# Filter transform: two stacked products become one of 128 columns; the last chunk is scored by VectorE

## The chip, the cores and the metric

One core of a Trainium2 chip runs the whole program. The metric is the device time of one execution in microseconds; a kernel is judged by the median of several executions. TensorE multiplies matrices out of on-chip memory into its accumulators (PSUM, eight banks), VectorE (DVE), ScalarE (ACT) and GpSimd (POOL) do elementwise work, and SyncE (SP) issues most of the transfers to and from device memory. All data are float32.

## The reference

A long convolution with a gate, followed by a small mixture of experts. The filter is made from a table of positions by two small products, then windowed.

```python
h_filt = (np.maximum(pos_emb @ w1, 0.0) @ w2) * np.exp(-0.01 * pos)[:, None]
u = x * v
Hf = np.fft.rfft(h_filt, n=2 * S, axis=0)             # S = 12608, 128 channels
Uf = np.fft.rfft(u, n=2 * S, axis=1)                  # 4 batches
y = np.fft.irfft(Uf * Hf[None], n=2 * S, axis=1)[:, :S]
x = x * y
# per batch: the 128 rows with the highest scores go through one expert
scores = np.einsum('bsd,d->bs', x, w_gate)
top = np.argpartition(-scores[b], 128)[:128]
out[b, top] = x[b, top] + sigmoid(scores[b, top]) * (np.maximum(x[b, top] @ w1, 0) @ w2)
```

## The kernel before

The transforms are done as real (Hartley) transforms of length 101 x 250, written as matrix products. Channels go through in 32 groups of four (`NG`), and everything is placed by hand: buffers lie at fixed offsets of one large tile (`arena`, another is `big`), and each engine works its instructions off in the order in which the program issues them. There is no scheduler and no table that sets the order.

**The filter** comes first. `h_hid` makes it in `big` (`hb`: 101 rows, two versions e = 0 and 1, 128 channels, 126 columns). `h_spec` then transforms it, group by group, and writes the spectrum to device memory (`hd`, L409), from where the main loop reads it for each batch. A group passes through these steps:

- `fold` (L365): the 126 columns are folded about their middle, sum and difference of column j and column 125 - j, for both e and four channels: two operations of 504 elements a row. VectorE does the first four groups, GpSimd the rest, four groups ahead, in four buffers (`fbo`).
- `fwd`, the first stage (L380): for each e and channel two products of 101 rows, 63 columns of weights (the folded filter) and 101 moving columns (`c1_sb`), one for rows 0 to 62 of the output, the other for rows 64 to 126. Which of the two, sum or difference, stands above is exchanged between e = 0 and 1 (`w ^ e`), so that for the second stage all that goes to p is above and all that goes to q below. Then ScalarE copies the two outputs to `te` (L383).
- The second stage (L400): for two halves of the moving columns, e and w, a product of 63 rows, 64 columns of weights (`fo_sb`, a table of cosines and sines) and 202 moving columns: eight a group. Row half w goes to bank p or q, e to the column half.
- ScalarE copies q (L402), VectorE makes the spectrum in four operations of 404 (L405, L406, twice L408), and SP sends it off (L409). The buffer written by L408 is one of two, so that L408 waits for the transfer of two groups before.

On TensorE, `fwd` of group g + 1 stands ahead of the second stage of group g. PSUM is double-buffered for both stages: the first uses banks a0 and a1 for even groups and c1 for odd ones, the second c2 and c0.

**The main loop** (128 steps, four batches of 32 groups) does the same for the input: `f_s1` (L424) and `dft` (L266) on TensorE, the product with the spectrum on VectorE (L430 to L445), `f_sd` on GpSimd, the way back `f_i` (L261) on TensorE.

**At the end of a batch** `P1.run` finishes the convolution in 32 steps h over the rows of the output (`mm`: L541, L545), multiplies by x (`fin`: L556) and scores. For scoring a chunk of up to four positions is multiplied by the gate vector (`weigh`, L590, by VectorE or, where `far`, by GpSimd) and ScalarE sums each position (`sums`, L600). In the last batch only, the last step (h = 31, two positions) is scored in one operation a position by VectorE (L574), under `end`. In that batch PSUM banks rotate among three (`ring`), h = 30 in a0, h = 31 in a1; the first expert's products for three batches (`Experts.half`, through L257) go to a0 and then a1 right behind, then eight warming products (L794), four products of the second expert layer (L257), and then the first count of the search for the 128 highest scores, which goes on in 16 rounds between VectorE and TensorE. A product is two records, each with its weight load, in the trace.

Of the kernel before, what the change touches and what calls it, by code (L numbers as in the profile page):

```python
# [17 lines left out]
B, S, D, FO = 4, 12608, 128, 64  # L18
NQ = 64
# [20 lines left out]
JH = (N3 + 1) // 2  # L40
# [51 lines left out]
def _tables():  # L92
    kap = np.arange(N1) - N1 // 2
    idx = _grid()
    r1, r3 = idx[:, 0] % N1, idx[0] % N3
    rho, chi = (-1.0) ** np.arange(N1), (-1.0) ** (np.arange(N3) + r3)
    c1 = np.zeros((128, 1 + NB, N1))
    c1[:N1, 0] = _cas(r1[:, None] * kap[None, :], N1)
    alt = rho[:, None] * c1[:N1, 0]
    for k, (c, lo, hi) in enumerate(_steps()[1]):  # L100
        c1[:hi, 1 + k], c1[hi:N1, 1 + k] = alt[:hi], -alt[hi:]
        c1[N1:N1 + hi - lo, 1 + k] = -2 * alt[lo:hi]
    g = _cas(kap[:, None] * N2 * np.arange(GW)[None, :], N1)
    gx = _split(np.concatenate([g, -g], axis=1))
    r = np.arange(NK)
    cf = np.zeros((N3, 2, 2, NQ))
    for e in range(2):
        ang = 2.0 * np.pi * ((r3[:, None] * (2 * r + e)[None, :]) % N2) / N2
        cf[:, 0, e, :NK] = np.cos(ang)
        cf[:, 1, e, :NK] = np.sin(ang)  # L110
    j = np.arange(NJ)
    ci = np.zeros((128, 2, NJ))
    for e in range(2):
        k = 2 * r + e
        wk = np.where((k == 0) | (k == N3), 0.5, 1.0)[:, None] / (2 * N)
        ang = 2.0 * np.pi * ((k[:, None] * j[None, :]) % N2) / N2
        ci[e * NQ:e * NQ + NK, 0] = np.cos(ang) * wk
        ci[e * NQ:e * NQ + NK, 1] = np.sin(ang) * wk
    fold = np.zeros((128, 2, NQ))
    fold[:JH] = cf[:JH, 0]  # L120
    fold[NQ:NQ + JH] = cf[:JH, 1]
    cf[:, :, 1] *= chi[:, None, None]
    win = np.exp(np.float32(-0.01) * np.arange(N1 * N3, dtype=np.float32))
    sg = np.where(idx % N2 < N3, 1.0, -1.0).astype(np.float32)
    wm = np.zeros((PR, 3, N3), np.float32)
    wm[:N1, 0] = np.where(idx < S, win[idx], 0.0)
    wm[:N1, 1] = sg
    wm[:, 2] = wm[:, 0] * wm[:, 1]
    p = np.arange(128)
    tk = np.zeros((128, 2 * 128 + 2 + 36 + NJ + 40), np.float32)  # L130
    tk[:, :128] = p[:, None] < p[None, :]
    tk[:, 128:256] = p[None, :]
    tk[:, 256] = NJ * np.clip(p - P0, 0, PR - 1)
    tk[:, 257] = p + 1
    steps = np.array([[i << sh for i in range(4)] for sh in range(14, -1, -2)])
    steps = np.concatenate([steps, steps[:1] - 32768])
    tk[:, 258:294] = steps.reshape(1, -1)
    tk[:, 294 + NJ:] = np.concatenate([-steps[:8], 0.5 - steps[8:], 0.5 - steps[:1]]).reshape(1, -1)
    tk[:, 294:294 + NJ] = np.where(_valid(), -NEG, NEG)
    f = np.float32  # L140
    cf = np.concatenate([cf.reshape(N3, 4, NQ), np.zeros((128 - N3, 4, NQ))])
    return (fold.astype(f), c1.astype(f), gx.astype(f), cf.astype(f), ci.astype(f), wm, tk)
# [18 lines left out]
def hyena_moe(ctx, tc, xg, x2, pos, bw, ww, wg, mw1, mw2, fo, c1, gx, cf, ci, wm, tk, out):  # L161
# [61 lines left out]
    nc.vector.memset(onesb, 1.0)  # L223
    ay = view(big, 0, [128, NG, 2 * NJ, 4])
    hb = view(big, 0, [N1, 2, D, N3 + 1])
    fo_sb = view(arena, OFF["wx"][0] + 32 * JH, [128, 2, NQ])
    fbo = [OFF["wx"][0], OFF["wx"][0] + 16 * JH] + [OFF["xa"][0] + k * 8 * D for k in (2, 3)]
    hd = dp.tile([128, NG, 2 * HC], F32, name="hd")
    blk = [c for c, _, _ in _steps()[1]]

# [121 lines left out]
    def h_spec():  # L352
        te = {}

        def tps(g):
            if g % 2:
                t = ps2(1, [128, 2, 512], f"htp_{g}")
                return [t[:, e, :HC] for e in range(2)]
            return [ps1(e, [128, HC], f"htp_{g}_{e}") for e in range(2)]

        def pqs(g):
            t = ps2(0 if g % 2 else 2, [128, 2, 512], f"hpq_{g}")
            return [t[:, e, :HC] for e in range(2)]

        def fold(g, eng=nc.gpsimd):  # L365
            if g >= NG:
                return
            fb[g] = view(arena, fbo[g % 4], [N1, 2, 2, 4, JH])
            hg = hb[:, :, 4 * g:4 * g + 4]
            for k, op in enumerate((ALU.add, ALU.subtract)):  # L370
                eng.tensor_tensor(out=fb[g][:, k], in0=hg[:, :, :, :JH], in1=hg[:, :, :, N3:JH - 1:-1], op=op)

        def fwd(g):
            b = fb.pop(g)
            tp = tps(g)
            t = te[g] = buf("te", g, [128, 2, HC])
            for e in range(2):
                for s in range(4):
                    for w in range(2):
                        nc.tensor.matmul(tp[e][w * NQ:w * NQ + JH, s * N1:(s + 1) * N1], lhsT=b[:, w ^ e, e, s], rhs=c1_sb[:N1, 0],  # L380
                                         start=True, stop=True)
            for e in range(2):
                nc.scalar.copy(out=t[:, e], in_=tp[e])  # L383
            fold(g + 4)

        fb = {}
        for g in range(4):
            fold(g, nc.vector)
        fwd(0)
        for g in range(NG):  # L390
            if g + 1 < NG:
                fwd(g + 1)
            p, q = pqs(g)
            t = te.pop(g)
            for h in range(2):
                c = slice(h * 2 * N1, (h + 1) * 2 * N1)
                for e in range(2):
                    for w, o in enumerate((p, q)):
                        r = slice(w * NQ, w * NQ + JH)
                        nc.tensor.matmul(o[e * NQ:(e + 1) * NQ, c], lhsT=fo_sb[r, e], rhs=t[r, e, c], start=True, stop=True)  # L400
            qs = buf("qs", g, [128, HC])
            nc.scalar.copy(out=qs, in_=q)  # L402
            vs = buf("yz", g, [128, HC])
            ht = buf("sd", g, [128, 2, HC])
            nc.vector.tensor_tensor(out=nat(vs), in0=rev(p), in1=nat(qs), op=ALU.subtract)  # L405
            nc.vector.tensor_tensor(out=nat(p), in0=nat(p), in1=rev(qs), op=ALU.add)  # L406
            for e, op in enumerate((ALU.add, ALU.subtract)):
                nc.vector.tensor_tensor(out=ht[:, e], in0=p, in1=vs, op=op)  # L408
            nc.sync.dma_start(hd[:, g], ht.rearrange("p e c -> p (e c)"))  # L409
            if NG - 5 <= g < NG - 3:  # L410
                stage_u(g - NG + 5)
                load_u(g - NG + 7)
            if g == NG - 2:
                stage_u(2)
            if g >= NG - 3:
                load_h(g - NG + 3)
# [83 lines left out]
    class P1:  # L500
# [47 lines left out]
        def fin(self, h):  # L548
            ja, n = self.hbs[h]
            blk = ja // 8  # L550
            xa = self.xa[blk]
            js = slice(ja % 8, ja % 8 + n)
            end = self.last and n == 2
            if end:
                self.weigh()
            nc.vector.tensor_tensor(out=xa[:, js], in0=self.s4.pop(h)[:, :n], in1=xa[:, js], op=ALU.mult)  # L556
            if not end:
                self.weigh()
                far = ja >= JM and n == HB and h not in DW
                if h >= NL and not self.last:  # L560
                    o = OFF["cm"][0] + 2 * NC * D if h < 30 else OFF["wx"][0]
                    wx = view(arena, o + h % 2 * HB * D, [128, HB, D])
                elif far:
                    wx = view(arena, CE[self.pw % 2], [128, HB, D])
                    self.pw += 1
                else:
                    wx = view(arena, self.wx[self.nw % 4], [128, HB, D])
                    self.nw += 1
                self.mul = xa[:, js], wx[:, :n], ja, n, far, h
                if far:  # L570
                    self.weigh()
            else:
                for k in range(n):
                    nc.vector.scalar_tensor_tensor(out=junk, in0=xa[:, ja % 8 + k], scalar=1.0,  # L574
                                                   in1=self.wg, op0=ALU.mult, op1=ALU.mult,
                                                   accum_out=self.sc[:, ja + k:ja + k + 1])
            if ja + n == blocks[blk][1]:
                j0, j1 = blocks[blk]
                nc.sync.dma_start(out[self.b, :, j0:j1], xa[P0:P0 + PR, :j1 - j0])
                i = ORD.index(blk)  # L580
                if i:
                    self.load_a(i - 1 + NX + len(XE))
                if blk in CB:
                    self.comb()
# [573 lines left out]
```

## Time and profile before

| | |
|---|---|
| median of three executions | 905.29 us (904.11 to 909.53) |
| profiled execution | 909.53 us, span 907.8 us |
| busy of the span | TensorE 869.9 us (96%), VectorE 808.5 (89%), GpSimd 763.5 (84%), ScalarE 626.6 (69%) |
| filter made (`h_hid`) | up to about 34.7 us |
| filter transformed (`h_spec`) | 34.7 to about 120.5 us |
| main loop with the ends of the first three batches | to about 840 us |
| end of the fourth batch, search, experts | to 907.8 us |

The profiled execution is the longest of the three; the profile's times are of this one. In the lines of the profile, a line starts with the source line, the engine and the operation, then the tile written, an arrow and the tiles read, the shape (for a product: rows of weights x columns of weights, then rows and columns moving), and the number of instructions; behind a bar stand busy time in us, the mean of one in ns and the idle time just before with what ended it. Timeline lines start with start and length in us. `PEld` is TensorE's loading of weights, which can run beside its products; ends of products are modelled. "c", "a", "arena", "big" are the tiles of the program without their numbers.

### The profile page before, as it was taken

How to read it: one execution, taken by the hardware profiler on the slowest of the kernel's cores; microseconds unless marked ns; L12 is line 12 of the kernel's file. 1: busy time of each engine (PE TensorE's matmuls, PEld its weight loads, DVE VectorE, ACT ScalarE, POOL GpSimd, SP SyncE). 2: the span in 40 equal slices, each digit the busy share in tenths (PEclk: the TensorE clock that was granted, in tenths of full speed). 3: DMA queues.
4: the chain of work that ended last, by engine and by line, in shares of the span. 5: the costliest groups of instructions: out<-in, count | busy, mean ns of one | idle time of the engine just before them, and what ended most of it. 6: DMA issues, size and time to landing. Idle time of an engine off the chain costs nothing.

```text
span 907.8 us, 46386 instructions
## 1 busy us (share of the span) xinstructions
PE 869.9 (96%) x19606; PEld 760.9 (84%) x19606; DVE 808.5 (89%) x1543; ACT 626.6 (69%) x2238; POOL 763.5 (84%) x834
## 2 busy tenths in 40 slices
PE   8999989999999999999999999999999999999965
PEld 5777758999999879788898798897997888979954
DVE  7988889999999799999997899999988999997883
ACT  6655565555558788885578788865698888656920
POOL 5888649999999789998997799999997999889710
PEclk9999999999999999999999999999999999999997
DMA  7044596677887877678778776788798666755910
GB/s 247 21 169 166 189 305 208 214 221 222 262 247 232 280 237 226 201 206 251 237 225 279 248 225 200 222 230 247 230 283 288 207 215 209 239 181 180 294 45 7
DMA packets 83032, 195.06 MB, mean 215 GB/s; under 512 B 9579, under 2 KB 46548, under 8 KB 82824
## 3 DMA queue, kind: packets, MB, share of 16 engines
q1 hardware_dynamic: 82568, 191.57, 66.9%
q8 instruction: 154, 2.52, 1.1%
q0 software_dynamic: 256, 0.52, 0.2%
q14 instruction: 54, 0.44, 0.2%
HBM read 151.46 MB, written 40.60 MB: 212 GB/s over the span
## 4 chain that ended last, share of the span: by engine, by line
PE 62%; DVE 18%; DMA 8%; ACT 6%; issue 3%; POOL 2%; POOLq 0%; SPq 0%; DVEq 0%; ACTq 0%
PE c L261 20%; PE a L424 16%; PE c L266 16%; ACT arena L600 4%; DMA hd<-arena 4%; DVE arena L408 3%; PE c L545 2%; DMA out_dram<-arena 2%; PE a L541 2%; PE a L545 2%; DMA arena<-in_x_dram 2%; DVE arena L438 2%; DVE c L439 2%; PE c L541 1%; DVE ms L694 1%
## 5 line engine op out<-in xcount | busy, mean ns | idle before, releaser
L261 PE MATMUL c<-ci_sb,arena 128*26 128x126 f32 (+1 forms) x8128 | 260.6, 271 | 3.9 <-DVE arena L556 2.7
L261 PEld LDWEIGHTS c<-ci_sb,arena 128*26 128x26 f32 (+1 forms) x8128 | 243.0, 104 | 8.8 <-DVE arena L556 3.2
L266 PE MATMUL c<-arena,cf_sb 128*32 128x404 f32 x2048 | 213.0, 505 | 6.5 <-DVE arena L864 2.2
L424 PE MATMUL a<-c_sb,arena 128*32 128x202 f32 (+1 forms) x4096 | 214.8, 334 | 0.0
L424 PEld LDWEIGHTS a<-c_sb,arena 128*32 128x32 f32 (+1 forms) x4096 | 173.5, 108 | 28.1 <-issue 12.8
L247 POOL TENSOR_TENSOR arena<-arena 128x500 f32<-128x500 f32 x128 | 161.7, 1263 | 10.7 <-DMA arena<-in_xg_dram 10.7
L426 ACT COPY arena<-a 128x404 f32<-128x404 f32 x256 | 127.8, 499 | 53.3 <-PE a L424 52.4
L475 ACT COPY big<-c 128x824 f32<-128x824 f32 x127 | 106.3, 837 | 78.3 <-PE c L261 78.0
L451 POOL TENSOR_TENSOR arena<-arena 128x404 f32<-128x404 f32 x127 | 123.8, 975 | 39.7 <-DVE arena L445 28.5
L600 ACT ACTIVATE arena<-arena 128x128 f32<-128x128 f32 x502 | 147.4, 295 | 11.5 <-DVE arena L590 10.6
L266 PEld LDWEIGHTS c<-arena,cf_sb 128*32 128x32 f32 x2048 | 98.9, 109 | 41.7 <-issue 24.0
L438 DVE TENSOR_TENSOR arena<-c,arena 128x808 f32<-128x808 f32 x127 | 126.8, 999 | 5.3 <-ACT c L756 1.6
L439 DVE TENSOR_TENSOR c<-c,arena 128x808 f32<-128x808 f32 x127 | 126.7, 998 | 0.0
L452 POOL TENSOR_TENSOR arena<-arena 128x404 f32<-128x404 f32 x127 | 123.3, 971 | 0.0
L600 ACT ACTIVATION_READ_ACCUMULATOR arena<-arena 128x1 f32 x502 | 94.0, 187 | 0.0
L528 POOL TENSOR_TENSOR arena<-big 128x512 f32<-128x512 f32 x72 | 89.6, 1278 | 0.7 <-PE c L541 0.4
L269 ACT COPY arena<-c 128x404 f32<-128x404 f32 x128 | 63.5, 496 | 34.9 <-PE c L266 29.4
L433 DVE TENSOR_TENSOR c<-c,arena 128x404 f32<-128x404 f32 x128 | 74.7, 584 | 12.7 <-ACT arena L269 8.4
L444 DVE TENSOR_TENSOR arena<-c,arena 128x404 f32<-128x404 f32 x127 | 73.6, 579 | 12.9
L495 POOL TENSOR_TENSOR big<-big,arena 128x184 f32<-128x184 f32 x128 | 74.3, 580 | 10.0
L430 DVE TENSOR_TENSOR c<-c,arena 128x404 f32<-128x404 f32 x128 | 74.9, 585 | 2.7
L494 POOL TENSOR_TENSOR big<-big,arena 128x184 f32<-128x184 f32 x128 | 74.8, 584 | 0.6 <-ACT arena L476 0.6
(195 smaller groups left out, 1399.1 us busy)
## 6 DMA issues: line engine op xcount, KB each, us to landing
arena<-in_xg_dram SPq DMA_DIRECT2D x256, 250.0 KB, 3.6
arena<-hd SPq DMA_DIRECT2D x128, 404.0 KB, 4.1
out_dram<-arena SPq DMA_DIRECT2D x60, 420.0 KB, 5.8
arena<-in_x_dram SPq DMA_DIRECT2D x40, 420.0 KB, 4.9
hd<-arena SPq DMA_DIRECT2D x32, 404.0 KB, 3.0
arena<-in_x_dram SPq DMA_DIRECT2D x40, 210.0 KB, 4.7
arena<-in_pos_dram SPq DMA_DIRECT2D x15, 202.0 KB, 4.5
arena<-in_x_dram SPq DMA_DIRECT2D x4, 315.0 KB, 4.3
```

Of the source, the lines that this page charges most:

```text
L247: nc.gpsimd.tensor_tensor(out=x, in0=x, in1=v, op=ALU.mult)
L261: nc.tensor.matmul(o[32 * k:32 * k + c.stop - c.start], lhsT=lhsT[:, c], rhs=rhs, start=True, stop=True)
L266: nc.tensor.matmul(pq[w][a:a + 32], lhsT=cf_sb[:, 2 * w + a // NQ, a % NQ:a % NQ + 32], rhs=te[:, a // NQ], start=True, stop=True)
L424: nc.tensor.matmul(tps[s // 2][c, s % 2], lhsT=u[:, s, c], rhs=c1_sb[:, 0:k + 2:k + 1], start=True, stop=True)
L426: nc.scalar.copy(out=te[:, :, 2 * h:2 * h + 2].rearrange("p e s i -> p s e i"), in_=tps[h])
L438: nc.vector.tensor_tensor(out=mt, in0=uv, in1=ht[:, 0].unsqueeze(1).to_broadcast([128, 2, HC]), op=ALU.mult)
L439: nc.vector.tensor_tensor(out=uv, in0=uv, in1=ht[:, 1].unsqueeze(1).to_broadcast([128, 2, HC]), op=ALU.mult)
L451: eng.tensor_tensor(out=nat(sd[:, 0]), in0=nat(yz[:, 0]), in1=rev(yz[:, 1]), op=ALU.add)
L452: eng.tensor_tensor(out=nat(sd[:, 1]), in0=rev(yz[:, 0]), in1=nat(yz[:, 1]), op=ALU.subtract)
L475: nc.scalar.copy(out=ay[:, t % NG, :NJ + JM, ss], in_=o3[:, :, :NJ + JM].rearrange("p s x -> p x s"))
L528: nc.gpsimd.tensor_tensor(out=cm[:, e].rearrange("p j (g s) -> p j g s", s=4), in0=av[0], in1=av[1], op=op)
L600: nc.scalar.activation(out=x, in_=x, func=AF.Copy, accum_out=self.sc[:, j:j + 1])
```

## The change

Two things are changed. In `h_spec` the folded filter of one e and channel now lies as 128 neighbouring columns, the sum in the first 64 and the difference in the last 64 (63 + 1 each; the added column multiplies nothing in the second stage), and one product of 128 columns does what two products of 63 did. The sum is now above for both e; so the second stage picks its row half by `w ^ e`, its table (`fold`) is laid out to match, and it runs over all 404 moving columns at once. Folds have 512 elements a row instead of 504, written in runs of 64. In `P1.fin`, `end` now holds for the last two steps of the last batch: step 30 too is scored by VectorE, in four operations, instead of by GpSimd and ScalarE.

```diff
     fold = np.zeros((128, 2, NQ))
-    fold[:JH] = cf[:JH, 0]
-    fold[NQ:NQ + JH] = cf[:JH, 1]
+    for e in range(2):
+        for w in range(2):
+            fold[w * NQ:w * NQ + JH, e] = cf[:JH, w ^ e, e]
...
-            fb[g] = view(arena, fbo[g % 4], [N1, 2, 2, 4, JH])
+            fb[g] = view(arena, fbo[g % 4], [N1, 2, 4, 2 * NQ])
             hg = hb[:, :, 4 * g:4 * g + 4]
             for k, op in enumerate((ALU.add, ALU.subtract)):
-                eng.tensor_tensor(out=fb[g][:, k], in0=hg[:, :, :, :JH], in1=hg[:, :, :, N3:JH - 1:-1], op=op)
+                eng.tensor_tensor(out=fb[g][:, :, :, k * NQ:(k + 1) * NQ], in0=hg[:, :, :, :NQ], in1=hg[:, :, :, N3:N3 - NQ:-1], op=op)
...
             for e in range(2):
                 for s in range(4):
-                    for w in range(2):
-                        nc.tensor.matmul(tp[e][w * NQ:w * NQ + JH, s * N1:(s + 1) * N1], lhsT=b[:, w ^ e, e, s], rhs=c1_sb[:N1, 0],
-                                         start=True, stop=True)
+                    nc.tensor.matmul(tp[e][:, s * N1:(s + 1) * N1], lhsT=b[:, e, s], rhs=c1_sb[:N1, 0], start=True, stop=True)
...
-            for h in range(2):
-                c = slice(h * 2 * N1, (h + 1) * 2 * N1)
-                for e in range(2):
-                    for w, o in enumerate((p, q)):
-                        r = slice(w * NQ, w * NQ + JH)
-                        nc.tensor.matmul(o[e * NQ:(e + 1) * NQ, c], lhsT=fo_sb[r, e], rhs=t[r, e, c], start=True, stop=True)
+            for e in range(2):
+                for w, o in enumerate((p, q)):
+                    r = slice((w ^ e) * NQ, (w ^ e) * NQ + JH)
+                    nc.tensor.matmul(o[e * NQ:(e + 1) * NQ], lhsT=fo_sb[r, e], rhs=t[r, e], start=True, stop=True)
...
-            end = self.last and n == 2
+            end = self.last and h >= len(self.hbs) - 2
             if end:
                 self.weigh()
             nc.vector.tensor_tensor(out=xa[:, js], in0=self.s4.pop(h)[:, :n], in1=xa[:, js], op=ALU.mult)
```

The changed file is three lines shorter from the first stage on, so L400 becomes L397, L556 becomes L553 and so on. On TensorE, in the filter's transform, the rows of an even and an odd group (a_70, a_71 and c_73 are the first stage's banks, c_74 and c_72 the second's) stand before like this:

```order
L400 MATMUL c_74<-arena 64x202 x8
L380 MATMUL a_70<-c_sb,arena 63x101 x8
L380 MATMUL a_71<-c_sb,arena 63x101 x8
L400 MATMUL c_72<-arena 64x202 x8
L380 MATMUL c_73<-c_sb,arena 63x101 x16
```

and in the changed kernel like this (columns of weights x moving columns, and the count):

```order
L397 MATMUL c_74<-arena 64x404 x4
L380 MATMUL a_70<-c_sb,arena 128x101 x4
L380 MATMUL a_71<-c_sb,arena 128x101 x4
L397 MATMUL c_72<-arena 64x404 x4
L380 MATMUL c_73<-c_sb,arena 128x101 x8
```

The order of the stages is the same; each has half the products, with twice the columns of weights in the first and twice the moving columns in the second. On VectorE, at the end of the last batch, the rows from step 29 on (c_72, a_70 and a_71 are the banks of steps 29, 30 and 31, c_73 holds the gate vector) stand before like this:

```order
L556 TENSOR_TENSOR arena<-c_72,arena 128x512
L590 TENSOR_TENSOR arena<-arena,c_73 128x512
L556 TENSOR_TENSOR arena<-a_70,arena 128x512
L590 TENSOR_TENSOR arena<-arena,c_73 128x512
L556 TENSOR_TENSOR arena<-a_71,arena 128x256
L574 SCALAR_TENSOR_TENSOR arena,sc_12823<-arena,c_73 128x128 x2
```

and in the changed kernel like this:

```order
L553 TENSOR_TENSOR arena<-c_72,arena 128x512
L587 TENSOR_TENSOR arena<-arena,c_73 128x512 x2
L553 TENSOR_TENSOR arena<-a_70,arena 128x512
L571 SCALAR_TENSOR_TENSOR arena,sc_12439<-arena,c_73 128x128 x4
L553 TENSOR_TENSOR arena<-a_71,arena 128x256
L571 SCALAR_TENSOR_TENSOR arena,sc_12439<-arena,c_73 128x128 x2
```

The weighing of step 29 has moved ahead of the product that reads a_70, and four scorings stand between that and the product that reads a_71. On GpSimd one product of 512 and on ScalarE four sums are gone there. On TensorE the end of the last batch keeps its order; with the engines waited for it stands in the changed kernel like this (the last is the second expert layer; DVE is VectorE, DMAHW a transfer):

```order
L538 MATMUL a_71<-big,gx_sb 64x128 [waits DVE_49]
L538 MATMUL a_71<-big,gx_sb 64x128 x3
L258 MATMUL a_70<-arena 64x128 [waits DMAHW2_49,DVE_49,Activation_49]
L258 MATMUL a_70<-arena 64x128 x7
L258 MATMUL a_71<-arena 64x128 [waits DVE_49]
L258 MATMUL a_71<-arena 64x128 x7
L791 MATMUL c_72<-ident 128x128 x8
L258 MATMUL c_72<-arena 64x128 [waits DMAHW4_49,DMAHW3_49,Activation_49]
```

The expert's products into a_70 and a_71 wait for the VectorE products that read these banks, and the warming products and the second layer are queued behind them.

More of the change, by code (lines that the diff above doesn't have):

```diff
@@ L225, in hyena_moe @@
     hb = view(big, 0, [N1, 2, D, N3 + 1])
-    fo_sb = view(arena, OFF["wx"][0] + 32 * JH, [128, 2, NQ])
-    fbo = [OFF["wx"][0], OFF["wx"][0] + 16 * JH] + [OFF["xa"][0] + k * 8 * D for k in (2, 3)]
+    fo_sb = view(arena, OFF["wx"][0] + 32 * NQ, [128, 2, NQ])
+    fbo = [OFF["wx"][0], OFF["wx"][0] + 16 * NQ] + [OFF["xa"][0] + k * 8 * D for k in (2, 3)]
     hd = dp.tile([128, NG, 2 * HC], F32, name="hd")
```

## The prediction

> **What bounds the kernel now.** I read the page first, then the stretch in which the filter is transformed, because most of the diff is there: its sum by engine, its groups by shape, its waits, and TensorE's timeline of single groups.
>
> ```profile
> span 907.8 us, 46386 instructions
> 34.70:115.20 80.50, 76.89 (x1537) 62.22 (x1536) 71.17 (x129) 45.13 (x95) 62.02 (x58) 1.00 0.42 159
> L408 DVE TENSOR_TENSOR arena<-c,arena 128x404 f32<-128x404 f32 x60 | 31.9, 573 | 7.8 <-DMA hd<-arena 7.0
> L406 DVE TENSOR_TENSOR c<-c,arena 128x404 f32<-128x404 f32 x31 | 18.2, 586 | 1.1
> L405 DVE TENSOR_TENSOR arena<-c,arena 128x404 f32<-128x404 f32 x31 | 17.7, 571 | 0.5
> L371 POOL TENSOR_TENSOR arena<-big 101x504 f32<-101x504 f32 x56 | 59.6, 1089 | 12.2 <-PE a L380 5.0 <-PE c L380 3.7 <-DVE arena L371 3.5
> DVE arena L408 <- DMA hd<-arena: 8.9, 8, 1.5
> PE c L400 <- DVE arena L408: 2.0, 2, 1.1
> ```
>
> The second line is the stretch from the first filter product to the last: 80.5 us, then busy time of TensorE, its weight loads, VectorE, ScalarE and GpSimd, the granted clock (1.00) and the DMA share. Thirty-two groups of four channels pass through it. VectorE needs 571 + 586 + 2 x 573 = 2303 ns for a group and sits idle 8.9 us in all, for the write of the spectrum two groups back, whose buffer it wants. GpSimd needs 2 x 1.09 = 2.18 us, ScalarE three copies. TensorE's pace stands in its timeline.
>
> ```profile
> 68.47 1.61 PE L380 MATMUL a<-c_sb,arena 101*63 101x101 f32 x32
> 70.01 0.92 PE L400 MATMUL c<-arena 63*64 63x202 f32 x16
> 70.85 1.61 PE L380 MATMUL c<-c_sb,arena 101*63 101x101 f32 x32
> 72.39 0.92 PE L400 MATMUL c<-arena 63*64 63x202 f32 x16
> ```
>
> Columns are start, length, line and count; a product of the program is two records here. First stage to second is 1.54 us, second to first 0.84, so a group is 2.38 us of TensorE, and the bursts stand back to back. 32 x 2.38 = 76.2 us of the 80.5: TensorE waits only about 4.3 us in the stretch, part of it at the start, part when VectorE is held up by its DMA. The two engines run almost level, VectorE with its DMA wait a little behind. A faster TensorE would gain little; a TensorE slower by more than 0.13 us a group (4.3 / 32) would set the pace.
>
> **The first stage: eight products of 128 columns.** Sixteen products of 63 columns, two at a time in the two halves of the columns, become eight of 128; the moving operand stays 101 wide. What changes is the weight load: its length grows with columns, and the two halves no longer load beside each other.
>
> ```profile
> L380 PEld LDWEIGHTS a<-c_sb,arena x512: 132/136/136, 34.7 to 109.5; 101*63 101x63 f32 x171
> L319 PEld LDWEIGHTS c<-c_sb x32: 163/169/169, 31.7 to 34.4; 101*101 101x101 f32 x32
> L794 PEld LDWEIGHTS c<-ident x16: 186/192/192, 862.5 to 864.2; 128*128 128x128 f32 x16
> L380 PE MATMUL a<-c_sb,arena x512: 250/250/301, 34.7 to 109.6; 101*63 101x101 f32 x171
> L794 PE MATMUL c<-ident x16: 275/275/377, 862.5 to 864.3; 128*128 128x128 f32 x16
> 31.69 2.93 PEld L319 LDWEIGHTS c<-c_sb 101*101 101x101 f32 x32
> 862.49 1.86 PEld L794 LDWEIGHTS c<-ident 128*128 128x128 f32 x16 [0.17 <-issue]
> 862.50 2.05 PE L794 MATMUL c<-ident 128*128 128x128 f32 x16
> ```
>
> Loads of 63, 101 and 128 columns last 136, 169 and 192 ns: 0.86 ns a column. The warming bursts have the new form, untiled with a load for each record. L319, 101 columns and 101 moving, starts its 32 loads in 2.93 - 0.17 = 2.76 us, 89 ns each (31 gaps). L794, 128 columns and 128 moving, starts 16 in 1.86 - 0.19 = 1.67 us, 111 ns each (15 gaps); its first product starts with its first load, and its last 2.05 - 0.275 = 1.775 us after that. The new burst is also 16 records; it has L794's load and L319's moving operand, so its starts take between 16 x 89 ns = 1.42 us and L794's 1.775. The old burst's take 1.61 - 0.25 = 1.36 us. Hence +0.06 to +0.415 us a group. I take 0.415: from 101 to 128 columns the spacing grows by 111 - 89 = 22 ns and the load by 192 - 169 = 23 ns, as if the next load must end before the next product starts. The other reading, that the 128 moving columns make those 22 ns, is the low end.
>
> A rule of the Trainium skill speaks against the change more strongly: TensorE: Matmul & The Clock Gate, Part 3 (What overlaps and what doesn't), says that a weight load overlaps a running product only if it goes to another row group. By that, load and product of the untiled burst would alternate. The two warming bursts use all row groups again and again and start a record every 89 and 111 ns, less than the 169 and 192 ns that one load lasts, so the trace does not agree; the case stays below as a rival.
>
> **The second stage: four products of 404.** Eight products of 202 become four, on the same four 64 x 64 tiles; now both row halves write each PSUM bank, in different partitions. The form is in the trace: L307, 64 rows, 64 columns, 404 moving, with its row half and column half exchanged for the second bank.
>
> ```profile
> 11.88 0.91 PE L307 MATMUL c<-arena 64*64 64x404 f32 x8
> 12.72 0.36 PE L329 MATMUL c<-arena 64*101 64x128 f32 x2
> ```
>
> From its first record to the next burst's is 0.84 us, as for L400 above. Cost: 0 (-0.02 to +0.02 a group). The Trainium skill, TensorEngine Tiling (Array Packing), Gotcha 1: PSUM Pressure, says different row tiles cannot write one PSUM bank at once; L307's 0.84 us for eight records does not show it.
>
> **Fold.** GpSimd's folds grow from 504 to 512 elements with an output in runs of 64: 1.09 x 512/504 = 1.11 us, 2.21 a group. Even at the length of its other additions of 512 (1278 ns, below) it is 2.56, under TensorE's new 2.80. VectorE's eight opening folds lengthen by the same share, about 0.1 us in all, before TensorE needs them.
>
> ```profile
> L528 POOL TENSOR_TENSOR arena<-big 128x512 f32<-128x512 f32 x72 | 89.6, 1278 | 0.7 <-PE c L541 0.4
> hd<-arena SPq DMA_DIRECT2D x32, 404.0 KB, 3.0
> ```
>
> **Sum of the stretch.** A group is now 2.38 + 0.415 = 2.80 us of TensorE, over VectorE's 2.30. The write of a spectrum then has 2 x 2.80 - 1.15 = 4.45 us instead of 2 x 2.30 - 1.15 = 3.45 before its buffer is wanted (1.15 are the two L408), against a median landing of 3.0, so that wait mostly goes and what is late next is TensorE itself, without a stop: 34.7 + 32 x 2.80 = 124.3 for the end of its filter work.
>
> ```profile
> 115.20 1.58 PE L424 MATMUL a<-c_sb,arena 128*32 128x202 f32 x32
> 121.06 1.56 PE L266 MATMUL c<-arena,cf_sb 128*32 128x404 f32 x16 [0.66 <-DVE c L433]
> 119.08 0.49 ACT L269 COPY arena<-c 128x404 f32<-128x404 f32 x1 [1.68 <-PE c L266]
> 120.42 0.58 DVE L433 TENSOR_TENSOR c<-c,arena 128x404 f32<-128x404 f32 x1
> ```
>
> Before, the first input product (L424) starts at 115.20; now at 124.3, +9.1. Does the hand-over absorb any? VectorE starts the first input group at 120.42 though ScalarE gave it its data at 119.6, so VectorE's own path shifts by only about 8.3. But TensorE's path from L424 onward (its bursts, ScalarE's copies between them, the next group) has no slack that I can see, and from 125 us on TensorE leads the loop. So +9.1, and +8.3 if VectorE's start is what counts.
>
> **The tail.** The last chunk of four positions is scored by four VectorE operations instead of one GpSimd product and four ScalarE sums.
>
> ```profile
> 859.21 0.68 DVE L590 TENSOR_TENSOR arena<-arena,c 128x512 f32<-128x512 f32 x1
> 859.80 0.68 DVE L556 TENSOR_TENSOR arena<-a,arena 128x512 f32<-128x512 f32 x1
> 861.00 0.42 DVE L556 TENSOR_TENSOR arena<-a,arena 128x256 f32<-128x256 f32 x1
> 861.52 0.29 DVE L574 SCALAR_TENSOR_TENSOR arena<-arena,c 128x128 f32<-128x128 f32 x1
> 861.85 0.29 DVE L574 SCALAR_TENSOR_TENSOR arena<-arena,c 128x128 f32<-128x128 f32 x1
> 862.74 1.36 ACT arena L600 x9
> 864.13 0.30 DVE sc L604
> 860.56 1.76 PEld L257 LDWEIGHTS a<-arena 128*64 128x64 f32 x32 [1.01 <-ACT arena L600]
> 861.47 0.85 PEld L257 LDWEIGHTS a<-arena 128*64 128x64 f32 x16
> 862.50 2.05 PE L794 MATMUL c<-ident 128*128 128x128 f32 x16
> 864.63 1.09 PE L257 MATMUL c<-arena 128*64 128x128 f32 x16
> 866.24 0.20 PE L257 MATMUL c<-st,onesb 128*64 128x3 bf16 x2 [0.52 <-DVE ms L697]
> ```
>
> ScalarE ends its sums at 864.10 and VectorE masks at 864.13. Four sums fewer, each 0.29 us from start to start, end at 862.93. VectorE: L590 of the chunk before moves up to 859.80, L556 to 860.40, then four scorings 0.33 us apart from 861.19, L556 of the last two positions at about 862.45, ended by 862.9, two scorings to 863.6. The mask comes at about 863.6: -0.5 us. But L556 also frees the PSUM banks into which the first expert's products go. In the second load row the second half starts at 861.47, when L556 (861.00 + 0.42) has ended; it would now start at about 862.95. The warming burst behind it on TensorE starts 1.03 later (861.47 to 862.50), so at 863.97; the next expert product follows a whole burst, 1.96 after that (2.05, less the 0.07 to 0.09 by which bursts overlap above), at 865.93, and the count of the first round, which stands behind its 16 records (0.85 to 0.9), at about 866.8 instead of 866.24. The mask is early, the count is late: +0.5 us, bounds -0.5 (if TensorE is not late) and +1.
>
> **Sum.** The profiled execution took 909.5 us (its span is 907.8). 909.5 + 9.1 + 0.5 = 919.1 for an execution like it. It is the longest of the three before, and 4.2 above their median 905.3; on the median, 905.3 + 9.6 = 914.9. I forecast 915. Were the 4.2 us longer DMA waits in this stretch, which vanish in the changed kernel, the true loss would be larger, up to 919.
>
> **Rivals.** *The load stays hidden* (not slower): the spacing follows the moving operand, 89 ns, so a group is 2.38 + 0.06 = 2.44 us, inside the 2.51 (80.5 / 32) that it has. TensorE uses up to 32 x 0.06 = 1.9 us of its slack; with the tail -0.5 to +0.5 the time is 905 to 907. It decides below +0.13 us a group. For it: one burst of products alone cannot part the two readings. Against: 22 ns and 23 ns above. Chance 0.10. *Load and product alternate*, by the rule on row groups: a load of about 110 ns (0.86 x 128) and a product of about 85 by turns are 195 ns, 16 of them 3.1 us, +1.75 a group, 32 x 1.75 - 4.3 = +52: about 957. Chance 0.03. *The banks collide* in the second stage: the row halves by turns would double most of the 0.84 us, about 0.7 a group, 32 x 0.7 = 22 us on top of the forecast: about 937. Chance 0.03. That the VectorE scoring does not do what it says is inside the tail's bounds.
>
> **Chances.** My forecast has 0.84. Its own range is 912 (the hand-over absorbs 0.8, the tail gains 0.5, the executions scatter by a microsecond or two) to 920. A change of about 1%, 9 us, is what a measurement of this kernel can tell from none; the forecast lies just past it, so 0.84 splits into 0.50 slower and 0.34 same. The first rival adds 0.08 same and 0.02 faster, the two others 0.06 slower. The range 909 to 920 leaves out the rivals (0.16) and little else.
>
> **What would show it.** Right: loads of about 192 ns at L380, its bursts 1.96 us to the next burst, 2.80 us a group, VectorE idle in every group for TensorE by way of ScalarE instead of the DMA, the first input product near 124 us; in the tail the mask before 864 minus the shift, and the first count waiting on TensorE. Wrong: a group still at 2.44 us, VectorE's DMA waits still there and the end near 115; or a second stage longer than 0.9 us.

## The result and the profile after

The changed kernel takes 919.8 us (median of four executions, 915.8 to 923.4), the kernel before 906.9 in the same comparison: 1.0142 times as long, with a 95% interval from 1.0113 to 1.0172, so 10 to 16 us more. The forecast was 915 (range 909 to 920), 9.6 above the 905.3 that the kernel before then had. The profiled execution took 915.8 us with a span of 914.0; it is the shortest of the four, while the one profiled before is the longest of its four, so the two spans lie only 6.2 us apart and are compared here stretch by stretch.

| us | before | after |
|---|---|---|
| up to the first filter product | 34.7 | 33.6 |
| the filter's transform, up to the first input product | 80.5 | 89.7 |
| from there to VectorE's product of step 29 in the last batch | 743.4 | 741.3 |
| from there to the end | 49.2 | 49.4 |

No edit of this document touches the code of the third row, and of the first only VectorE's opening folds (0.1 us). Yet over the thirteen profiled executions (all but the one with half the moving columns) the first takes 32.9 to 35.7 us and the third 739.1 to 745.2. So the time of one whole execution can hide or feign a few microseconds of loss, and the lengths of the changed stretches are the better measure.

The stretch of the filter's transform, in the same views as before: its sum by engine, VectorE's groups and the waits of VectorE.

```profile
33.50:123.30 89.80, 89.43 (x768) 66.16 (x768) 72.73 (x128) 45.06 (x95) 64.06 (x59) 1.00 0.38 146
L405 DVE TENSOR_TENSOR arena<-c,arena 128x404 f32<-128x404 f32 x60 | 31.9, 573 | 1.6 <-DMA hd<-arena 0.6
L402 DVE TENSOR_TENSOR arena<-c,arena 128x404 f32<-128x404 f32 x31 | 17.9, 578 | 14.3 <-ACT arena L399 14.3
L403 DVE TENSOR_TENSOR c<-c,arena 128x404 f32<-128x404 f32 x30 | 17.6, 587 | 1.0
DVE arena L402 <- ACT arena L399: 14.3, 29, 0.8
```

VectorE has the same work (573, 578, 587 ns), but what it waits for has changed. The wait for the transfer is down from 8.9 us to 0.6, and in 29 of 32 groups VectorE now waits for ScalarE's copy of a TensorE result, 14.3 us in all. TensorE is busy 89.43 of 89.80 us. Its timeline and the loads, at the same place as before:

```profile
68.11 0.91 PE L397 MATMUL c<-arena 63*64 63x404 f32 x8
68.95 2.03 PE L380 MATMUL c<-c_sb,arena 101*128 101x101 f32 x16
70.91 0.91 PE L397 MATMUL c<-arena 63*64 63x404 f32 x8
68.95 1.86 PEld L380 LDWEIGHTS c<-c_sb,arena 101*128 101x128 f32 x16 [0.63 <-issue]
L380 PEld LDWEIGHTS a<-c_sb,arena x256: 186/192/192, 33.6 to 118.2; 101*128 101x128 f32 x128
```

A group is 70.91 - 68.11 = 2.80 us instead of 2.38. The second stage to the next burst is 0.84 as before; the first stage is 1.96 instead of 1.54. Sixteen loads take 1.86 us, just as long as the sixteen of the warming burst L794 that moved 128 columns, though here 101 are moved: (1.86 - 0.19) / 15 = 111 ns.

At the hand-over to the main loop (TensorE; L421 is L424 of before, L267 is L266):

```profile
122.47 0.91 PE L397 MATMUL c<-arena 63*64 63x404 f32 x8 [0.28 <-ACT arena L382]
123.31 1.58 PE L421 MATMUL a<-c_sb,arena 128*32 128x202 f32 x32
125.56 1.56 PE L267 MATMUL c<-arena,cf_sb 128*32 128x404 f32 x16 [0.66 <-ACT arena L423]
129.17 1.56 PE L267 MATMUL c<-arena,cf_sb 128*32 128x404 f32 x16 [0.66 <-ACT arena L423]
```

The first input product starts at 123.31 instead of 115.20, and the second L267 at 129.17 instead of 121.06: +8.1 at both, nothing is absorbed. The stretch begins 1.1 us earlier in this execution (33.6 against 34.7), so it is 89.7 us long against 80.5, +9.2.

In the tail (first two rows of before, VectorE's product of step 29 and the operation that takes up the first count; then VectorE's timeline and TensorE's loads after):

```profile
858.60 0.69 DVE L556 TENSOR_TENSOR arena<-c,arena 128x512 f32<-128x512 f32 x1 [0.69 <-PE c L541]
866.48 0.18 DVE st L714 x2
864.59 0.69 DVE L553 TENSOR_TENSOR arena<-c,arena 128x512 f32<-128x512 f32 x1 [0.46 <-PE c L538]
866.39 0.68 DVE L553 TENSOR_TENSOR arena<-a,arena 128x512 f32<-128x512 f32 x1
867.18 0.29 DVE L571 SCALAR_TENSOR_TENSOR arena<-arena,c 128x128 f32<-128x128 f32 x1
868.38 0.42 DVE L553 TENSOR_TENSOR arena<-a,arena 128x256 f32<-128x256 f32 x1
869.56 0.29 DVE L601 TENSOR_TENSOR sc<-sc,tk_sb 128x126 f32<-128x126 f32 x1
873.02 0.16 DVE L711 SCALAR_TENSOR_TENSOR st<-c,tk_sb 128x3 f32<-128x3 f32 x1 [1.26 <-PE c L258]
868.85 0.85 PEld L258 LDWEIGHTS a<-arena 128*64 128x64 f32 x16 [0.83 <-DVE arena L553]
869.88 1.86 PEld L791 LDWEIGHTS c<-ident 128*128 128x128 f32 x16 [0.17 <-issue]
871.86 0.85 PEld L258 LDWEIGHTS c<-arena 128*64 128x64 f32 x16
```

Counted from the product of step 29 (864.59; before 858.60), the mask (L601, before L604) comes after 4.97 us instead of 5.53, and the operation that takes up the first count (L711, before L714) after 8.43 instead of 7.88. VectorE stands idle 1.26 us before it, for TensorE. From the mask to the count it is 3.46 us instead of 2.35. That difference is the firmer one: in the eight profiled executions with the tail of before, the mask itself comes 5.27 to 5.92 us after the product, but the count always 2.34 to 2.35 after the mask.

### The profile page after: what moved, and what is told of

Read it like the earlier page. It is cut to its first block, busy times and chain, and to the rows that moved or that the text cites. A ratio compares the mean times of both kernels' runs of the same rounds, so it can differ in the third digit from the quotient of the medians.

```text
span 914.0 us, 44824 instructions
## 1 busy us (share of the span) xinstructions
PE 879.2 (96%) x18838; PEld 761.5 (83%) x18838; DVE 812.2 (89%) x1551; ACT 625.4 (68%) x2230; POOL 764.1 (84%) x833
## 4 chain that ended last, share of the span: by engine, by line
PE 68%; DVE 11%; ACT 7%; DMA 6%; POOL 5%; issue 3%; POOLq 0%; SPq 0%; DVEq 0%; ACTq 0%
PE c L262 18%; PE a L421 16%; PE c L267 16%; ACT arena L597 5%; DMA out_dram<-arena 4%; PE a L380 3%; PE c L380 3%; PE c L397 3%; PE a L542 2%; PE c L542 1%; PE a L538 1%; DMA arena<-in_x_dram 1%; DVE arena L435 1%; DVE c L436 1%; POOL arena L525 1%
## 5 line engine op out<-in xcount | busy, mean ns | idle before, releaser
L267 PE MATMUL c<-arena,cf_sb 128*32 128x404 f32 x2048 | 213.3, 503 | 7.3 <-ACT arena L423 3.0
L421 PE MATMUL a<-c_sb,arena 128*32 128x202 f32 (+1 forms) x4096 | 215.6, 334 | 0.0
L421 PEld LDWEIGHTS a<-c_sb,arena 128*32 128x32 f32 (+1 forms) x4096 | 171.9, 108 | 29.8 <-issue 12.8
L267 PEld LDWEIGHTS c<-arena,cf_sb 128*32 128x32 f32 x2048 | 98.6, 109 | 43.0 <-issue 26.0
L525 POOL TENSOR_TENSOR arena<-big 128x512 f32<-128x512 f32 x72 | 89.6, 1279 | 0.7 <-PE c L538 0.4
L441 DVE TENSOR_TENSOR arena<-c,arena 128x404 f32<-128x404 f32 x127 | 73.6, 579 | 12.9
L492 POOL TENSOR_TENSOR big<-big,arena 128x184 f32<-128x184 f32 x128 | 74.4, 581 | 10.0
L372 POOL TENSOR_TENSOR arena<-big 101x512 f32<-101x512 f32 x56 | 60.9, 1090 | 19.9 <-PE a L380 10.8
```

Of the source, the lines that this page charges most:

```text
L267: nc.tensor.matmul(pq[w][a:a + 32], lhsT=cf_sb[:, 2 * w + a // NQ, a % NQ:a % NQ + 32], rhs=te[:, a // NQ], start=True, stop=True)
L421: nc.tensor.matmul(tps[s // 2][c, s % 2], lhsT=u[:, s, c], rhs=c1_sb[:, 0:k + 2:k + 1], start=True, stop=True)
L525: nc.gpsimd.tensor_tensor(out=cm[:, e].rearrange("p j (g s) -> p j g s", s=4), in0=av[0], in1=av[1], op=op)
```

## The experiments

All are measured against the kernel before in the same comparison; a ratio is given with its 95% interval. In the intervals, 0.001 is about 0.9 us.

**The filter's part alone.**

```diff
-            end = self.last and h >= len(self.hbs) - 2
+            end = self.last and n == 2
```

> The filter's part of the change alone; the last chunk is scored as before. Theory (the weight load of 128 columns sets a spacing of 111 ns, TensorE needs 2.80 us a group and sets the pace): groups of 2.80 us, the first input product 8 to 9 us later than before, the median 8 to 9 us above the kernel before. Rival A (the loss beyond 9.6 us comes from the tail): the same here, and the tail alone costs 3 us more. Rival B (a usual execution before has fewer waits of VectorE for its transfer than the profiled one, so that the filter costs more): here already 11 to 13 us.

Measured: 918.9 us against 906.9, ratio 1.0127 (1.0086 to 1.0168), 8 to 15 us. The groups are 2.80 us.

```profile
70.93 0.91 PE L397 MATMUL c<-arena 63*64 63x404 f32 x8
71.77 2.03 PE L380 MATMUL a<-c_sb,arena 101*128 101x101 f32 x16
73.73 0.91 PE L397 MATMUL c<-arena 63*64 63x404 f32 x8
123.52 1.58 PE L421 MATMUL a<-c_sb,arena 128*32 128x202 f32 x32
```

The first input product is at 123.52, 8.3 later than in the profiled execution before. The filter carries the loss. The time cannot tell the theory's 8 to 9 us from rival B's 11 to 13: the interval takes in both.

**The tail's part alone.**

```diff
-            end = self.last and n == 2
+            end = self.last and h >= len(self.hbs) - 2
```

> The scoring of step 30 by VectorE alone; the filter as before. Theory (the mask comes 0.5 us earlier, but the product that frees the second expert's bank is queued behind four scorings, and the first count comes later): the mask 0.5 us earlier and the count 0.5 us later against the last weighing, the whole 0.5 us slower, hardly measurable. Rival A (the tail holds the rest of the loss): 3 us slower. Rival C (TensorE is not late): 0.5 us faster.

Measured: 907.2 against 906.9, ratio 1.0006 (0.9980 to 1.0031). The trace shows both halves of the theory.

```profile
852.00 0.68 DVE L556 TENSOR_TENSOR arena<-c,arena 128x512 f32<-128x512 f32 x1
855.78 0.42 DVE L556 TENSOR_TENSOR arena<-a,arena 128x256 f32<-128x256 f32 x1
856.97 0.29 DVE L604 TENSOR_TENSOR sc<-sc,tk_sb 128x126 f32<-128x126 f32 x1
860.42 0.16 DVE L714 SCALAR_TENSOR_TENSOR st<-c,tk_sb 128x3 f32<-128x3 f32 x1 [1.25 <-PE c L257]
```

From step 29 the mask takes 4.97 us (5.53 before), the count 8.42 (7.88): 0.56 earlier, 0.54 later. Rival A, 3 us in the tail, falls: its 3 us lie just outside the interval (-1.8 to +2.8). Rival C, a gain of 0.5 us, is not excluded by the time, but the count is late in the trace.

**The first stage again as two products, of 64 columns.** Layout, fold and second stage stay as in the change.

```diff
-                    nc.tensor.matmul(tp[e][:, s * N1:(s + 1) * N1], lhsT=b[:, e, s], rhs=c1_sb[:N1, 0], start=True, stop=True)
+                    for w in range(2):
+                        r = slice(w * NQ, (w + 1) * NQ)
+                        nc.tensor.matmul(tp[e][r, s * N1:(s + 1) * N1], lhsT=b[:, e, s, r], rhs=c1_sb[:N1, 0], start=True, stop=True)
```

> The filter's part with the new layout, the new fold and the second stage of four products of 404, but with the first stage again as two products of 64 columns in the two column halves; the tail as before. Theory: the first stage's burst is 1.36 us again, a group 2.38 us, VectorE waits for its transfers again, the time is that of before within 1 us. Rival (the second stage's banks or the folds in runs of 64 carry the loss): groups stay above 2.6 us and the time stays 6 us or more above before.

Measured: 911.1 against 906.9, ratio 1.0049 (1.0024 to 1.0075), 2 to 7 us.

```profile
69.49 0.91 PE L399 MATMUL c<-arena 63*64 63x404 f32 x8
70.33 1.61 PE L382 MATMUL c<-c_sb,arena 101*64 101x101 f32 x32
71.86 0.91 PE L399 MATMUL c<-arena 63*64 63x404 f32 x8
DVE arena L407 <- DMA hd<-arena: 4.4, 5, 1.7
```

The mechanism is as expected: the burst is 1.61 us again, a group 2.37, and VectorE waits for its transfers. So the products of 128 columns are what makes a group 2.80. But the time does not come back to within 1 us of before, as was expected; some 4 us stay. The trace cannot show where: the profiled execution took 904.2 us, the shortest of twelve and less than the median before, and it reached the first input product at 113.09, earlier than the one profiled before.

**Half the moving columns.** Only 50 of the 101 columns are moved in the first stage, so half of its result is missing.

```diff
-                    nc.tensor.matmul(tp[e][:, s * N1:(s + 1) * N1], lhsT=b[:, e, s], rhs=c1_sb[:N1, 0], start=True, stop=True)
+                    nc.tensor.matmul(tp[e][:, s * N1:s * N1 + 50], lhsT=b[:, e, s], rhs=c1_sb[:N1, 0, :50], start=True, stop=True)
```

> As the filter's part alone, but the products of the first stage move only 50 of the 101 columns of the second operand (the other half of the first stage's result is left out). Theory (the load of 128 columns sets the spacing): 16 records still start in about 1.75 us, 111 ns each, a group is 2.7 to 2.8 us. Rival D (the moving operand sets it): records every 50 to 90 ns, the burst 0.9 to 1.4 us, a group 2.0 to 2.4 us, and VectorE sets the pace again.

Measured: 988.6 us, one execution. The loads at the start of the stretch and in its middle, the sums of two windows (length, then busy time of TensorE, loads, VectorE, ScalarE and GpSimd, then the granted clock), and the page's row of the granted clock (a digit is 24.7 us, in tenths):

```profile
33.43 1.86 PEld L380 LDWEIGHTS a<-c_sb,arena 101*128 101x128 f32 x16 [0.53 <-DVE arena L372]
69.43 3.49 PEld L380 LDWEIGHTS a<-c_sb,arena 101*128 101x128 f32 x16 [1.25 <-POOL arena L372]
33.00:36.00 3.00, 2.64 (x24) 2.57 (x24) 2.93 (x6) 0.99 (x2) 0.34 (x1) 1.00 0.00 0
60.00:80.00 20.00, 20.00 (x96) 14.64 (x95) 8.78 (x16) 5.36 (x12) 7.99 (x8) 0.50 0.21 84
PEclk9755555599999999999999999999999999999997
```

At the full clock sixteen loads take 1.86 us with 50 moving columns, as with 101 and with 128. That settles it: the load sets the spacing, and rival D falls. Nobody expected the rest: some four microseconds into the stretch the granted clock fell to 0.50 and stayed there up to the end of the stretch, near 195 us, and the loads took twice as long; in the main loop it is 1.00 again. The 988.6 us measure that clock, not the group that was forecast.

**The second stage alone, and the layout alone.** Two kernels part the 4 us that stayed. The first is the kernel before with the second stage as four products of 404 (its row half still w); the second is the kernel with two products of 64 columns, but with the second stage in eight products of 202. The first one's edit:

```diff
-            for h in range(2):
-                c = slice(h * 2 * N1, (h + 1) * 2 * N1)
-                for e in range(2):
...
+            for e in range(2):
+                for w, o in enumerate((p, q)):
+                    r = slice(w * NQ, w * NQ + JH)
+                    nc.tensor.matmul(o[e * NQ:(e + 1) * NQ], lhsT=fo_sb[r, e], rhs=t[r, e], start=True, stop=True)
```

> The kernel before with the second stage as four products of 404 and nothing else changed (old fold, first stage of two products of 63, old table). It parts the 4 us by which the kernel with two products of 64 stayed above before. Theory (the second stage costs nothing, 0.84 us as before): within 1 us of before. Rival (the longer products hold up ScalarE's copy of q or VectorE, and carry the 4 us): 3 to 5 us slower.

> New fold and layout with first-stage products of 64 columns, and the second stage as eight products of 202, its rows picked as in the changed kernel; the tail as before. Theory that the new fold carries the 4 us: 3 to 5 us slower than before. Rival (the second stage of 404 does): within 1 us of before. If neither this nor the second stage alone moves the time, it is their sum or the scatter between programs.

Measured: second stage alone 1.0027 (1.0000 to 1.0053), layout alone 1.0017 (0.9997 to 1.0038). In microseconds that is 0 to 5 and 0 to 3. Each touches no change at all with the low end of its interval, the middle of neither (2.4 and 1.5) is in the 3 to 5 us that would make it the one cause, and together the two middles are as much as the 4 us. Neither run decides by its time. In the traces the two stretches, from the first filter product to the first input product, are 83.2 and 80.0 us long. Kernels whose TensorE takes 2.38 us a group scatter there by the waits for the transfer: 80.5 before, 77.7 with the tail's part alone, 79.9 with two products of 64, 81.7 with the reordered tail below. So these 4 us can be put down to neither part and are seen in no line; they stay open.

**More buffers for the spectrum.** Four instead of two, on the kernel before.

```diff
+        hto = [OFF[k][0] + j * 2 * HC for k in ("sd", "cm") for j in range(2)]
...
-            ht = buf("sd", g, [128, 2, HC])
+            ht = view(arena, hto[g % 4], [128, 2, HC])
```

> The kernel before with four buffers for the spectrum on its way to device memory instead of two. Theory (before, the stretch is set by VectorE's waits for these transfers, TensorE has about 4 us of slack): VectorE's waits for the transfer go, TensorE runs at 2.38 us a group throughout, the first input product is 1 to 4 us earlier, and the whole 1 to 4 us faster. Rival (the transfers themselves set the pace): the waits move to another place, no gain.

Measured: 916.2 against 906.5, ratio 1.0089 (1.0060 to 1.0119). The two added buffers lay over the second stage's table and over a fold buffer, so that the spectrum is not the reference's, and engines waited for each other over what they covered. It says nothing on the question. The next run places two of the four elsewhere and uses `hto` in the same way:

```diff
+        hto = [OFF[k][0] for k in ("mt", "cm")] + [OFF["sd"][0] + j * 2 * HC for j in range(2)]
```

> The kernel before with four buffers for the spectrum, now all of them in memory that nothing else uses in this stretch. Theory (before, VectorE's waits for its transfers hold the stretch; TensorE has about 4 us of slack): the waits of VectorE for the transfer vanish, TensorE's groups are 2.38 us throughout, the first input product about 3 us earlier, the whole 1 to 4 us faster. Rival (the transfers set the pace): the waits move, no gain.

Here one of the added buffers still covered part of the second fold buffer (which a group's spectrum then overwrites, so the filter differs from the reference's); the memory was less free than the expectation says. The waits that matter can be read all the same.

```profile
107.90 0.92 PE L401 MATMUL c<-arena 63*64 63x202 f32 x16
109.51 0.92 PE L401 MATMUL c<-arena 63*64 63x202 f32 x16 [0.70 <-ACT arena L403]
110.36 1.58 PE L425 MATMUL a<-c_sb,arena 128*32 128x202 f32 x32
DVE arena L406 <- ACT arena L403: 0.3, 1, 0.3
```

The only wait of VectorE longer than 0.2 us in the stretch is 0.3 us for ScalarE; the wait for the transfer is gone, the first input product is at 110.36 and the stretch 77.2 us long, 2.41 a group. Measured: 903.5 against 906.4, ratio 0.9967 (0.9941 to 0.9993). So the stretch before was held by these waits, and TensorE had some 3 us of slack in it (80.5 - 77.2), as the prediction read it.

> The filter's part of the change (tail as before) with the same four buffers. Theory (TensorE's 2.80 us a group set the pace, the transfers have time enough): nothing changes, 8 to 13 us above before as without them. Rival (in usual executions of the changed kernel VectorE still waits for transfers, which is the part of the loss beyond the forecast): 3 us less than without them.

With the same buffers (and the same overlap) the filter's part of the change stays where it was: ratio 1.0138 (1.0104 to 1.0171) against 1.0127 without them, a stretch of 89.7 us as in the change. The two ratios come from two comparisons and are known to some 4 us each, so the times alone do not exclude the rival's 3 us. The traces do for the profiled executions: without the added buffers VectorE waits for a transfer 0.6 us in the change and 0.2 us in the filter's part alone, so there is no 3 us of it to gain. TensorE sets the pace there.

**The tail reordered.** The two products that free the experts' banks go first, then the weighing of step 29, then six scorings.

```diff
             end = self.last and h >= len(self.hbs) - 2
-            if end:
-                self.weigh()
...
+                if h + 1 == len(self.hbs):
+                    self.weigh()
+                    for j in range(blocks[blk][0], ja + n):
+                        nc.vector.scalar_tensor_tensor(out=junk, in0=xa[:, j % 8], ...)
```

> The filter as before; step 30 scored by VectorE as in the change, but the two products that free the experts' banks go first, then the weighing of step 29, then all six scorings. Theory (the changed tail loses because the product that frees the second bank stands behind four scorings): the mask 0.5 us earlier and the first count 0.3 to 0.6 us earlier too, the whole 0.3 to 0.6 us faster, less than can be told from the times alone. Rival: the count stays as late as in the change (0.5 us later).

Measured: 905.6 against 906.5, ratio 0.9981 (0.9957 to 1.0005). The trace shows it better than the time.

```profile
860.35 0.69 DVE L554 TENSOR_TENSOR arena<-c,arena 128x512 f32<-128x512 f32 x1 [0.69 <-PE c L541]
861.55 1.02 DVE L554 TENSOR_TENSOR arena<-a,arena 128x512 f32<-128x512 f32 x2
865.12 0.29 DVE L604 TENSOR_TENSOR sc<-sc,tk_sb 128x126 f32<-128x126 f32 x1
867.47 0.17 DVE L714 SCALAR_TENSOR_TENSOR st<-c,tk_sb 128x3 f32<-128x3 f32 x1
```

From step 29 the mask takes 4.77 us and the count 7.12, against 5.53 and 7.88 before: now both are 0.76 earlier, and the count follows 2.35 us behind the mask again. So the place of one product behind four scorings is what made the count late.

**Both gains together.** First with the four buffers:

> The kernel before with the four buffers and with the reordered tail (the two products that free the experts' banks first, then the weighing, then six scorings by VectorE). If both gains hold and add up: 2 to 5 us faster than before; in the tail the first count 7.1 us after the product of step 29 instead of 7.9.

Measured: 903.3 against 906.4, ratio 0.9962 (0.9941 to 0.9982), the count after 7.12 us (again with the overlapping buffer). The four buffers alone had 903.5 in the same comparison, so the tail's gain is seen in the trace and not in the time. Then with three buffers, the third being the main loop's `mt`, which nothing else touches in this stretch:

```diff
+        hto = [OFF["sd"][0], OFF["sd"][0] + 2 * HC, OFF["mt"][0]]
...
-            ht = buf("sd", g, [128, 2, HC])
+            ht = view(arena, hto[g % 3], [128, 2, HC])
```

> The kernel before with three buffers for the spectrum (the third is the main loop's first product buffer, which nothing uses in this stretch) and the reordered tail: the version that the runs point to. Theory: with three buffers a transfer has 3 x 2.38 - 1.15 = 6.0 us before its buffer is wanted, so VectorE's waits go as with four; the filter's stretch 77 us, the first count 7.1 us after the product of step 29, the whole 2 to 4 us faster than before. Rival (three are too few): the waits stay and only the tail's half microsecond is gained.

Measured: 901.7 against 904.6, ratio 0.9965 (0.9936 to 0.9994). VectorE no longer waits for a transfer, the stretch is 77.2 us, the count comes after 7.16 us. With the filter of before, this version beats the kernel before by 3 us (0.5 to 6), and so the changed kernel by some 16, which is a sum over two comparisons.

## Why the prediction was right, and where it fell short

**TensorE's slack.** Right. The prediction put 4.3 us of waiting into the old stretch, in part at its start, and 0.13 us a group as the point from which TensorE sets the pace. With the waits for the transfer gone the old products take 77.2 us instead of 80.5, so some 3 us of the 4.3 were these waits.

**The load of 128 columns.** Right in kind and size: of the two ends, +0.06 and +0.415 us a group, it took the upper because load and spacing grew by the same 22 to 23 ns. A group is 2.80, and a burst of sixteen loads takes 1.86 whether 50, 101 or 128 columns are moved. The first rival (0.10) is disproved by the short moving operand at full clock, the alternation of load and product (0.03), which needs 195 ns, by the 111 ns. Why the load has that spacing, "as if the next load must end before the next product starts", no run tests.

**The second stage and its banks.** The 0.84 us held, with both row halves writing one bank; that rival falls too. Whether four products of 404 cost anything elsewhere is open (1.0000 to 1.0053 alone).

**The folds.** Right: GpSimd's take 1072 ns at the median instead of 1066, VectorE's eight 692 instead of 677, and neither holds TensorE's pace.

**The sum of the stretch.** Forecast 89.6 us, measured 89.7; +9.1 forecast, +9.2 in length, +8.1 at its end, because this execution entered it earlier. The hand-over absorbs nothing.

**The tail.** Right up to the first count: the mask 0.56 us early (forecast 0.5), the count 0.55 late (forecast 0.56), and for the reason given, the second half of the first expert's products. The reordered tail shows it by taking that reason away. As a term of the sum the 0.5 us is not confirmed: from step 29 to the end it is 49.4 us in the change and 49.3 with the tail alone, within the 48.7 to 50.0 of the eight executions with the tail of before.

**The whole.** The forecast of 915 rests on a loss of 9.6 us; measured are 12.9 (10 to 16). That 919.8 still lies in the range of 909 to 920 is in part luck. Of the 4.8 us between forecast and measurement 1.6 are the kernel before, whose median was 905.3 when the forecast was made and 906.9 in the comparison; the other 3.3 are loss that the sum does not have. If they are more than scatter (the interval's low end is only 0.6 above the forecast loss, and the 8 to 15 us of the filter's part alone contain its 9.1), the term that was too small is the last one, "on the median": what the filter's part adds to a usual execution beyond TensorE's 9 us. The prediction offered a cause, and its upper end of 919 for it: that the 4.2 us of the profiled execution over the median were transfer waits that vanish. The runs do not bear that out. Six traces with the old pace have stretches of 77.7 to 83.2 us, 80.5 on average, so the profiled one was usual there, and more buffers leave the changed filter where it was. What the runs show in its place is that the kernel with the new layout and second stage but without the wide load still lies 2 to 7 us above before. So some 3 us may well not be the load's; which part makes them, or whether they are the scatter of one program against another, the runs do not settle.

## What to carry to other kernels

A product that fills all 128 columns loses what the column halves gave here, that their loads ran beside each other: the 32 loads of 63 columns, 136 ns each, took 1.41 us together, the 16 of 128 columns 1.86. With 50 or 101 moving columns the load then set the spacing, so before merging two narrow products into a wide one, look in a trace for the spacing of loads of the new width. When two engines run almost level, a shorter list of instructions is worth nothing until it is known which of them the stretch waits for. And before handing work to an engine, look at what frees a bank or a buffer behind it in that engine's queue: at the first count, order decided between 0.5 us lost and 0.8 us won here.

## What was not expected of the hardware

With 50 instead of 101 moving columns, TensorE's instruction stream was at first as dense as in the change, loads every 111 ns and products behind them. Yet some four microseconds into the stretch the granted clock fell from 1.00 to 0.50, and it stayed there until the stretch ended; sixteen loads then took 3.49 us instead of 1.86, so in this trace the load ran on the granted clock too. Less work in the products went with a whole program 70 us slower than the filter's part with all 101 columns (988.6 against 918.9). With 101 columns the same loads kept the full clock. This is one execution of one kernel: what the clock follows, and where between 50 and 101 columns it would change, was not tried.
